# A decoder block's forward and backward pass: V of seven groups kept on chip, moments centred in PSUM, gradients staged over V and K

## The chip, the cores and the metric

The kernel runs on one core of a Trainium2 chip. The metric is the device time of one execution in microseconds (us). The kernel before takes 814.06 us, the median of three runs (812.51 to 818.42). Engines are named PE (TensorE's matmuls), PEld (its weight loads), DVE (VectorE), ACT (ScalarE), POOL (GpSimd) and SP (SyncE). POOL and SP compute little here; their queues issue the transfers.

## What is computed

One token of 448 features passes through attention over a key and value cache and a gated layer without a nonlinearity; the outputs are the result and the gradients of eight inputs. Cut to what matters:

```python
def f(x, k_cache, v_cache, wq, wo, w_gate, w_up, w_down):
    q = layernorm(x) @ wq                       # 16 heads of 256, 8 groups of 2 heads
    k = k_cache[:, :, Sk - 4096:, :]            # Sk = 32768: the last 4096 rows of each group
    v = v_cache[:, :, Sk - 4096:, :]
    p = softmax(q @ k.T / 16)                   # per head
    h = x + (p @ v).reshape(1, 4096) @ wo
    n = layernorm(h)
    return h + ((n @ w_gate) * (n @ w_up)) @ w_down
out, vjp = jax.vjp(f, ...)
return out, *vjp(grad_out)
```

All is bf16. The gradients of the two caches have the full shape (8, 32768, 256): outside the last 4096 rows they are zero, and these zeros must be written. That is 235 MB of the 281 MB that the kernel writes.

## The kernel before

**Two streams of transfers.** SP's queue (`FILL`) writes the zeros from a constant tile, 14,336 KB at a time, from the start on, without waiting for anything computed (lines 57 to 75). The last region is cut into pieces (`CUT`, line 72): most of it from all 128 partitions, 63 rows of 16 KB from 3 partitions (`LOW3`), and on POOL's queue, after the load of the up weights (`fill_rest`, line 77), 176 rows of 16 KB from 8 partitions (`HIGH8`) and a little from `LOW8`. POOL's queue (`IO`) carries all other transfers, in the order of its program: loads of K, V and weights, and stores of gradients. A transfer that waits for a buffer holds up those behind it. The order on each engine is laid out by a scheduler that may pull later work ahead of work that waits.

**Memory.** `S` has eight slots of 16 KB per partition, each for one group's window of K or V (4096 rows of 256, 32 rows `t` per partition). `K_SLOT` and `V_SLOT` (lines 31 and 32) say which. V of groups 5, 6 and 7 takes slots that K or other data need again, so `V_AGAIN` loads them a second time in the backward stage. `Mt` holds the moments in fp32; `Rt` is a ring of scratch buffers and later holds weights.

**Forward stage**, per group g of 8 (lines 365 to 383): `scores` transposes K in TensorE (line 283), evacuates by `evac`, which gives its copies to ACT and DVE by turns (lines 227 and 229), and multiplies by q. `softmax` follows. `moments` (line 325) forms for every t the product of K's rows with the two heads' probabilities (DVE, line 335) and accumulates in PSUM V^T (p K), a 256 x 512 matrix (line 339), which serves dq later: the gradient of q needs V^T diag(p) K without its mean part, o times kbar, where o = V^T p and kbar = K^T p. o and kbar are accumulated by four 128 x 2 matmuls per t (lines 342 and 345). `load_K(g + 2)` and `load_V(g + 1)` are issued ahead of the group's work.

**Middle**: attention's output `ao` by wo (line 401), loaded in two halves `woA` and `woB`; the gated layer (line 411); `spread` (line 419) brings a column vector to all partitions for the products that give gradients (lines 441 and 453); `dq_ps` (line 471) multiplies the moments with the gradient of o, and the mean part kbar times delta is subtracted.

**Backward stage**, per group: V is transposed again (line 586), evacuated and multiplied by the gradient of o (line 591); from it come 32 rows for outer products (line 604); 16 times two matmuls give dV and dK for two t each (line 620), evacuated into two of the four staging slots `STG`, and stored (line 625). Between the groups the `side` jobs make the weight gradients: `outer` (line 494) multiplies a row by scalars into one of two staging buffers in `Mt` and stores it. `dxn_load` and `dxn_part` (lines 526 and 530) load wq again and reduce it for dx; `ffn_out` (line 515) loads w_down again and gives the block's output.

Of the kernel before, what the change touches and what calls it, by code (L numbers as in the profile page):

```python
# [26 lines left out]
NS = 8  # L27
NV = 5
# [6 lines left out]
K_SLOT = [5, 6, 7, 5, 6, 7, 5, 7]  # L35
V_SLOT = [0, 1, 2, 3, 4, 6, 6, 5]
V_AGAIN = {5: 1, 6: 2, 7: 3}
# [3 lines left out]
def kernel(  # L41
# [8 lines left out]
    small = ctx.enter_context(tc.tile_pool(name="small", bufs=2))  # L50
    ps = ctx.enter_context(tc.tile_pool(name="ps", bufs=1, space=bass.MemoryType.PSUM))

    x_bf = const.tile([1, D], bf16, tag="rowa", name="x_bf")
    FILL.dma_start(out=x_bf[:], in_=A_x.rearrange("a b d -> (a b) d"))
    go_bf = const.tile([1, D], bf16, tag="rowb", name="go_bf")
    FILL.dma_start(out=go_bf[:], in_=grad_out.rearrange("a b d -> (a b) d"))
# [15 lines left out]
    CUT = [n * ZW for n in (0, 640, 656, 719, 720, 896)]  # L72
    fill(FILL, last[CUT[2]:CUT[3]], LOW3, 21, ZW)
    fill(FILL, last[CUT[0]:CUT[1]], ALL, 5, ZW)
    fill(FILL, last[CUT[1]:CUT[2]], ALL, 1, ZW // 8)

    def fill_rest():
        fill(IO, last[CUT[3]:CUT[4]], LOW8, 2, 512)
        fill(IO, last[CUT[4]:CUT[5]], HIGH8, 22, ZW)


    S = const.tile([128, NS, SLOT], bf16)
    Mt = const.tile([128, G, 2, 2 * Dh], f32)
    Rt = const.tile([128, SLOT], bf16)

    def slot(k):
        return S[:, k, :]

    def slot_kv(k):
        return S[:, k, :].rearrange("p (t d) -> p t d", d=Dh)  # L90
# [17 lines left out]
    wq_sb = S[:, 1:3, :].rearrange("p a b -> p (a b)")[:, 0:NI * HQ]  # L108
# [4 lines left out]
    wd0 = S[:, 3, 0:FC * D].rearrange("p (c n) -> p c n", n=D)  # L113
    IO.dma_start(out=wd0, in_=B_w_down.rearrange("(c p) n -> p c n", p=128))

# [5 lines left out]
    ones_bf = const.tile([128, 128], bf16)  # L121
    V_.memset(ones_bf[:], 1.0)
    ones_f = const.tile([128, 128], f32)
    V_.memset(ones_f[:], 1.0)
    eps_t = const.tile([128, 1], f32)
# [35 lines left out]
    def rows_to_half(row, xe):  # L161
        t = ps.tile([128, NI], f32, tag="tmp", bufs=1)
        for i in range(NI):
            c = xe[i // 4][:, (i % 4) * 128:(i % 4 + 1) * 128]
            V_.tensor_copy(out=c.rearrange("o (m r) -> o m r", r=2), in_=half_cols(row, i))
            P_.matmul(t[:, i:i + 1], lhsT=c, rhs=ones_f[0:1, 0:1], start=True, stop=True)
        return t
# [64 lines left out]
    xe0 = [Mt[0:1, G - 1, k, :] for k in range(2)]  # L232
    xX = const.tile([128, NI], f32)
    V_.tensor_copy(out=xX[:], in_=rows_to_half(x_bf[:], xe0)[:])
    gX = const.tile([128, NI], f32)
    V_.tensor_copy(out=gX[:], in_=rows_to_half(go_bf[:], xe0)[:])
# [24 lines left out]
    kbar = const.tile([128, 32], f32)  # L261
# [4 lines left out]

    def kt_buf():
        k = kt_ctr[0] % NB
        kt_ctr[0] += 1
        return Rt[:, k * 1024:(k + 1) * 1024].rearrange("p (i h c) -> p i h c", i=4, h=2)  # L270

    def pk_buf():
        k = NB + pk_ctr[0] % NB
        pk_ctr[0] += 1
        return Rt[:, k * 1024:(k + 1) * 1024].rearrange("p (i h d) -> p i h d", i=2, h=2)
# [24 lines left out]
    def softmax(g):  # L300
# [19 lines left out]
        pf = small.tile([128, T, 2], f32, tag="p_f")  # L320
# [4 lines left out]
    def moments(g):  # L325

        K, Vv, pf = Kw[g], Vw[g], p_f[g]
        MT = fps.tile([128, 2, 2 * Dh], f32, tag="MT", name="MT")
        acc = fps.tile([128, 8], f32, tag="acc", name="acc")
        for c in range(T // 2):  # L330
# [5 lines left out]
            for i in range(2):  # L336
                t = 2 * c + i
                for hf in range(2):
                    P_.matmul(MT[:, hf, :], lhsT=Vv[:, t, hf * 128:(hf + 1) * 128], rhs=pk[:, i, :, :].rearrange("p h d -> p (h d)"),  # L339
                              start=(t == 0), stop=(t == T - 1))  # L340
                for hf in range(2):
                    P_.matmul(acc[:, 2 * hf:2 * hf + 2], lhsT=Vv[:, t, hf * 128:(hf + 1) * 128], rhs=pT_all[:, g, t, :],  # L342
                              start=(t == 0 and hf == 0), stop=(t == T - 1), skip_group_check=True)
                for dk in range(2):
                    P_.matmul(acc[:, 4 + dk:7 + dk:2], lhsT=K[:, t, dk * 128:(dk + 1) * 128], rhs=pT_all[:, g, t, :],  # L345
                              start=False, stop=(t == T - 1), skip_group_check=True)
        S_.copy(out=Mt[:, g, 0, :], in_=MT[:, 0, :])  # L347
        V_.tensor_copy(out=Mt[:, g, 1, :], in_=MT[:, 1, :])
        V_.tensor_copy(out=oT_f[:, 4 * g:4 * g + 4].rearrange("p (h f) -> p f h", f=2), in_=acc[:, 0:4].rearrange("p (f h) -> p f h", h=2))
        V_.tensor_copy(out=kbar[:, 4 * g:4 * g + 4], in_=acc[:, 4:8])  # L350
        V_.tensor_copy(out=oT_bf[:, 4 * g:4 * g + 4], in_=oT_f[:, 4 * g:4 * g + 4])

    wo_v = A_wo.rearrange("(b p) n -> p b n", p=128)
    woA = S[:, 6, 0:16 * D].rearrange("p (b n) -> p b n", n=D)
    woB = S[:, 5, 0:16 * D].rearrange("p (b n) -> p b n", n=D)
    wg_sb = S[:, 7, 0:NI * HF]
    wu_sb = Rt[:, 0:NI * HF]
    bc2 = [S[:, 7, NI * HF:NI * HF + F].rearrange("p (i c) -> p i c", i=2), Rt[:, NI * HF:NI * HF + F].rearrange("p (i c) -> p i c", i=2)]

    def wo_b(b):  # L360
        return woA[:, b, :] if b < 16 else woB[:, b - 16, :]
# [3 lines left out]
    for g in range(G):  # L365
        if g + 1 < NV:
            load_V(g + 1)
        if g + 2 < 7:
            load_K(g + 2)
        if g == 5:  # L370
            load_V(5)
        if g == 6:
            load_V(6)
            load_K(7)
        if g == 7:
            load_V(7)
            IO.dma_start(out=woA, in_=wo_v[:, 0:16, :])
        softmax(g)
        if g + 1 < G and g != 6:
            scores(g + 1)  # L380
        moments(g)
        if g == 6:
            scores(7)
        if g == 0:

            t = ps.tile([128, D], f32, tag="tmp", bufs=1)
            P_.matmul(t[:], lhsT=ones_bf[0:1, :], rhs=go_bf[:], start=True, stop=True)
# [4 lines left out]
    IO.dma_start(out=woB, in_=wo_v[:, 16:32, :])  # L392
# [6 lines left out]
    ao = ps.tile([1, D], f32, tag="tmp", bufs=1)  # L399
# [3 lines left out]
    V_.tensor_tensor(out=hX[:], in0=rows_to_half(ao[:], [S[0:1, k, 16 * D:SLOT].bitcast(f32) for k in (5, 6)])[:], in1=xX[:], op=ALU.add)  # L403
    rstd2, xh2, xf2, xx2 = layernorm(hX[:], "ln2")

    gu_ps = fps.tile([128, 2, 2, NI], f32, tag="sT", bufs=2)
# [12 lines left out]
    def spread(dst, src, nb, rows2):  # L419

        for b0 in range(0, nb, 4):
            n = min(4, nb - b0)
            t = fps.tile([2, 4, 128], f32, tag="sT", bufs=2, name="t")
            for j in range(n):
                P_.matmul(t[:, j, :], lhsT=src[:, b0 + j:b0 + j + nb + 1:nb], rhs=ident_bf[:], start=True, stop=True)
            evac(rows2[:, b0 * 128:(b0 + n) * 128].rearrange("p (b c) -> p b c", b=n), t[:, 0:n, :])
        for i2 in range(2):
            for b0 in range(0, nb, 4):
                n = min(4, nb - b0) * 128
                t = fps.tile([128, 512], f32, tag="sT", bufs=2, name="t")  # L430
                P_.matmul(t[:, 0:n], lhsT=Par[:, i2, :], rhs=rows2[:, b0 * 128:b0 * 128 + n], start=True, stop=True)
                evac(dst[:, i2, b0 * 128:b0 * 128 + n], t[:, 0:n])

    rows2 = [S[0:2, k, 16 * D:16 * D + HF] for k in (5, 6)]
    for w in range(2):
        spread(bc2[w], dgu[:, w, :], NI, rows2[w])
    P2 = const.tile([128, 2, NI], f32)
    for w, w_sb in ((0, wg_sb), (1, wu_sb)):
        wv = w_sb.rearrange("p (i c) -> p i c", i=NI)
        for i in range(NI):  # L440
            V_.tensor_tensor_reduce(out=wv[:, i, :], in0=wv[:, i, :], in1=bc2[w][:, i % 2, :], scale=1.0, scalar=0.0,  # L441
                                    op0=ALU.mult, op1=ALU.add, accum_out=P2[:, w, i:i + 1])
    dhn = const.tile([128, NI], f32)
    V_.tensor_tensor(out=dhn[:], in0=P2[:, 0, :], in1=P2[:, 1, :], op=ALU.add)
    dhZ = layernorm_bwd(dhn[:], xh2[:], rstd2[:, 0:1], gX[:], 0.5, "dhZ")

    dh_ps = fps.tile([128, D], f32, tag="sT", bufs=2)
# [18 lines left out]
    dq_ps = fps.tile([128, 32], f32, tag="acc", name="dq_ps")  # L466
    for h in range(H):
        for dk in range(2):
            for hf in range(2):
                c0 = (h % 2) * Dh + dk * 128  # L470
                P_.matmul(dq_ps[:, 2 * h + dk:2 * h + dk + 1], lhsT=Mt[:, h // 2, hf, c0:c0 + 128], rhs=doT_f[:, 2 * h + hf:2 * h + hf + 1],  # L471
                          start=(hf == 0), stop=(hf == 1))
    kd = small.tile([128, H, 2], f32, tag="kd")
    V_.tensor_tensor(out=kd[:], in0=kbar[:].rearrange("p (h f) -> p h f", f=2), in1=delta[:].unsqueeze(2).to_broadcast([128, H, 2]), op=ALU.mult)
    dqd = small.tile([128, 32], f32, tag="dqd")
    V_.tensor_tensor(out=dqd[:], in0=dq_ps[:], in1=kd[:].rearrange("p h f -> p (h f)"), op=ALU.subtract)
    dq = const.tile([128, 32], bf16)
    V_.tensor_scalar(out=dq[:], in0=dqd[:], scalar1=SCALE, scalar2=None, op0=ALU.mult)
    late = Mt[:].rearrange("p g f c -> p (g f c)").bitcast(bf16)
    dq_bc = late[:, 0:2 * HQ].rearrange("p (i c) -> p i c", i=2)  # L480
    spread(dq_bc, dq[:], 16, late[0:2, 4096:6144])
    fps_cm.__exit__(None, None, None)
    st_ctr = [0]

    def stage_buf():
        k = 1 + st_ctr[0] % 2
        st_ctr[0] += 1
# [170 lines left out]
```

## Time and profile before

| | |
|---|---|
| median of the runs | 814.06 us |
| the profiled execution, its own time | 811.53 us |
| its span | 809.8 us |
| bytes moved | 338.58 MB (read 57.28, written 280.59) |
| mean granted clock of TensorE | 0.644 |
| PE busy | 493.9 us (61%) |
| DVE busy | 378.3 us (47%) |
| ACT busy | 166.4 us (21%) |
| last moment matmul ends | 322 us |
| stores of dV and dK of group 0, issued | 532 us |
| of group 7, issued | 797 us |

The page cuts the span into 40 slices of 20.2 us; each digit is a busy share in tenths, DMA the mean share of the 16 DMA engines, and GB/s what they moved. Lists of waits give the waiting instruction, what released it, the total in us, how often, and the longest. A line number is one of the kernel; `evac`'s lines are shared by all that call it, and there the tile's name tells who did.

### The profile page before, as it was taken

The numbers are of one execution on the slowest core, as the hardware profiler recorded it, in microseconds if no ns is written. First come the engines' busy times: TensorE is split into PE (matmuls) and PEld (weight loads), VectorE is DVE, ScalarE is ACT, GpSimd is POOL, SyncE is SP. The second block draws the span as 40 slices with busy tenths as digits, with TensorE's granted clock in tenths as the row PEclk, the third lists the DMA queues.
The fourth block names the chain that finished last, engine by engine and source line by source line (L and its number), as shares of the span: only waits on it lengthen the run. The fifth ranks groups of instructions, "written<-read, shape, count | busy, mean of one in ns | idle before, by whom it ended". The sixth has DMA issues, their size and how long they took to land.

```text
span 809.8 us, 11007 instructions
## 1 busy us (share of the span) xinstructions
PE 493.9 (61%) x4479; PEld 294.7 (36%) x4479; DVE 378.3 (47%) x1149; ACT 166.4 (21%) x261; POOL 41.6 (5%) x77
## 2 busy tenths in 40 slices
PE   3559959999647529034597888687043454437742
PEld 3555536666324405012595774325031111001110
DVE  4128738777446306006674325683151463425532
ACT  0230111222000200001003332343011232224421
POOL 3000000000000001000000001010010110000000
PEclk9959688999778758665555556555555555555555
DMA  8999999999999999999999999999999999999996
GB/s 343 431 427 424 430 429 429 428 426 426 431 426 427 419 428 426 411 429 429 428 428 430 414 424 420 430 417 431 423 425 420 409 416 417 428 424 427 423 397 274
DMA packets 24920, 338.58 MB, mean 418 GB/s; under 512 B 1485, under 2 KB 1551, under 8 KB 5047
## 3 DMA queue, kind: packets, MB, share of 16 engines
q1 hardware_dynamic: 14550, 231.98, 67.8%
q0 software_dynamic: 10320, 105.90, 31.3%
q8 instruction: 35, 0.57, 0.3%
q14 instruction: 15, 0.12, 0.0%
HBM read 57.28 MB, written 280.59 MB: 417 GB/s over the span
## 4 chain that ended last, share of the span: by engine, by line
issue 24%; DMA 15%; PE 13%; DVE 7%; another core or an unknown queue 3%; POOL 1%; ACT 1%; POOLq 0%; ACTq 0%; DVEq 0%
DMA S<-in_A_v_cache_dram 5%; DMA S<-in_A_wo_dram 4%; DMA out_dram<-Mt 4%; PE dq_ps L471 3%; PE d_ps L620 2%; DMA Rt<-in_A_wq_dram 2%; DVE Rt L530 2%; PE MT L339 2%; DVE S L229 2%; PE tr L586 1%; ACT S L227 1%; DVE Rt L441 1%; POOL out_dram L495 1%; PE dh_ps L176 1%
## 5 line engine op out<-in xcount | busy, mean ns | idle before, releaser
L620 PE MATMUL d_ps<-R,Mt 32*128 32x512 bf16 x256 | 120.1, 605 | 102.6 <-DVE S L229 101.6
L339 PE MATMUL MT<-Rt,S 128*128 128x512 bf16 x512 | 147.6, 401 | 29.0 <-DMA S<-in_A_v_cache_dram 29.0
L335 DVE TENSOR_SCALAR Rt<-S,pf 128x256 bf16<-128x256 bf16 x512 | 117.5, 282 | 57.0 <-PE MT L339 50.3
L229 DVE CAST S<-d_ps 128x512 bf16<-128x512 f32 x128 | 86.6, 689 | 62.8 <-ACT S L227 37.0
L227 ACT CAST S<-d_ps 128x512 bf16<-128x512 f32 x128 | 74.8, 586 | 155.2 <-PE d_ps L620 152.9
L620 PEld LDWEIGHTS <-Mt 32*128 32x128 bf16 x256 | 26.4, 115 | 175.8 <-issue 173.4
L342 PEld LDWEIGHTS <-S 128*128 128x128 bf16 x512 | 49.3, 100 | 60.7 <-issue 9.4
L283 PE MATMUL tr<-ident_bf,S 128*128 128x128 bf16 x512 | 49.7, 256 | 34.0 <-DMA S<-in_A_k_cache_dram 29.6
L586 PE MATMUL tr<-ident_bf,S 128*128 128x128 bf16 x512 | 66.3, 307 | 1.9 <-ACT Mt L227 1.2
L586 PEld LDWEIGHTS <-S 128*128 128x128 bf16 x512 | 49.8, 139 | 9.6 <-issue 9.5
L283 PEld LDWEIGHTS <-S 128*128 128x128 bf16 x512 | 39.0, 116 | 32.5 <-DMA S<-in_A_k_cache_dram 30.0
L342 PE MATMUL acc<-pT_all,S 128*128 128x2 bf16 x512 | 48.2, 166 | 0.0
L345 PE MATMUL acc<-pT_all,S 128*128 128x2 bf16 x512 | 47.5, 164 | 0.0
L339 PEld LDWEIGHTS <-S 128*128 128x128 bf16 x512 | 33.8, 98 | 35.7 <-DMA S<-in_A_v_cache_dram 29.8
L227 ACT COPY Rt<-tr 128x1024 bf16<-128x1024 bf16 x32 | 32.4, 1012 | 65.3 <-PE tr L283 65.0
L227 ACT COPY Mt<-tr 128x1024 bf16<-128x1024 bf16 x32 | 32.4, 1013 | 62.0 <-PE tr L586 35.9
L347 ACT COPY Mt<-MT 128x512 f32<-128x512 f32 x8 | 4.7, 585 | 192.5 <-PE MT L339 165.2
L229 DVE COPY Mt<-tr 128x1024 bf16<-128x1024 bf16 x32 | 22.1, 690 | 41.6 <-PE tr L586 41.5
L401 PE MATMUL ao<-S,oT_bf 128*1 128x448 bf16 x32 | 9.4, 461 | 46.3 <-DMA S<-in_A_wo_dram 46.3
L229 DVE COPY Rt<-tr 128x1024 bf16<-128x1024 bf16 x32 | 22.1, 689 | 31.6 <-PE tr L283 30.4
L345 PEld LDWEIGHTS <-S 128*128 128x128 bf16 x512 | 31.0, 97 | 0.3 <-issue 0.3
L591 PEld LDWEIGHTS <-Mt 128*128 128x128 bf16 x512 | 20.2, 108 | 24.4 <-ACT Mt L227 12.5
(183 smaller groups left out, 451.5 us busy)
## 6 DMA issues: line engine op xcount, KB each, us to landing
out_dram<-zeros SPq DMA_DIRECT2D x15, 14336.0 KB, 148.9
out_dram<-S POOLq DMA_DIRECT2D x16, 2048.0 KB, 29.7
S<-in_A_v_cache_dram POOLq DMA_DIRECT2D x11, 2048.0 KB, 42.7
S<-in_A_k_cache_dram POOLq DMA_DIRECT2D x8, 2048.0 KB, 27.9
out_dram<-zeros SPq DMA_DIRECT2D x1, 10240.0 KB, 138.4
out_dram<-Mt POOLq DMA_DIRECT2D x6, 896.0 KB, 26.0
S<-in_A_wq_dram POOLq DMA_DIRECT2D x1, 3584.0 KB, 14.6
S<-in_A_wo_dram POOLq DMA_DIRECT2D x2, 1792.0 KB, 31.9
```

The lines of the kernel that those rows point to most:

```text
L227: S_.copy(out=out, in_=in_)
L229: V_.tensor_copy(out=out, in_=in_)
L283: P_.transpose(tr[:, i, dh, :], Xw[:, 4 * q + i, dh * 128:(dh + 1) * 128], ident_bf[:])
L335: V_.tensor_scalar(out=pk[:, i, h, :], in0=K[:, t, :], scalar1=pf[:, t, h:h + 1], scalar2=None, op0=ALU.mult)
L339: P_.matmul(MT[:, hf, :], lhsT=Vv[:, t, hf * 128:(hf + 1) * 128], rhs=pk[:, i, :, :].rearrange("p h d -> p (h d)"), start=(t == 0), stop=( ...
L342: P_.matmul(acc[:, 2 * hf:2 * hf + 2], lhsT=Vv[:, t, hf * 128:(hf + 1) * 128], rhs=pT_all[:, g, t, :], start=(t == 0 and hf == 0), stop=(t ...
L345: P_.matmul(acc[:, 4 + dk:7 + dk:2], lhsT=K[:, t, dk * 128:(dk + 1) * 128], rhs=pT_all[:, g, t, :], start=False, stop=(t == T - 1), skip_g ...
L471: P_.matmul(dq_ps[:, 2 * h + dk:2 * h + dk + 1], lhsT=Mt[:, h // 2, hf, c0:c0 + 128], rhs=doT_f[:, 2 * h + hf:2 * h + hf + 1], start=(hf = ...
L530: V_.tensor_tensor_reduce(out=wq2[:, i - i0, :], in0=wq2[:, i - i0, :], in1=dq_bc[:, i % 2, :], scale=1.0, scalar=0.0, op0=ALU.mult, op1=A ...
L586: P_.transpose(tr[:, i, dh, :], Vw[g][:, 4 * q + i, dh * 128:(dh + 1) * 128], ident_bf[:])
L591: P_.matmul(dp[:, 4 * q + i, :], lhsT=xt[:, i, dh, :], rhs=doT[:, 4 * g + dh:4 * g + dh + 3:2], start=(dh == 0), stop=(dh == 1))
L620: P_.matmul(d_ps[:, i, :, :].rearrange("p w d -> p (w d)"), lhsT=rows[32 * k:32 * k + 32, a, :], rhs=R[32 * k:32 * k + 32, :], start=True, ...
```

## The change

- V of groups 0 to 6 has a slot each, and is loaded once; V of group 7 takes a slot of K after `moments(6)` and is loaded again in the backward stage, after group 1's stores, into the slot of V of group 0. K has two slots by turns; `load_K(g + 2)` is issued after `moments(g)`. V of groups 1 and 2 is loaded with the first transfers, the next ones three groups ahead.
- One allocation `BIG` holds the slots and the scratch rings, with offsets by hand (`BASE`). `Mt` is bf16. `small` tiles have one buffer but for a few.
- In `moments` o and kbar come from one matmul per t, with the two probabilities as weights and V's and K's row of t side by side (two matmuls for groups 5 and 6, where the two slots are too far apart). Their product is subtracted in PSUM by two matmuls per group with a negated kbar, before `Mt` is evacuated, so that the subtraction after `dq_ps` goes.
- wo is loaded whole after the last moments, with w_gate and w_up behind it. `spread` leaves its result in PSUM, which the reductions read; ScalarE copies it to `bc2` afterwards.
- dV is staged over V of its group, dK over K's slot `g % 2`. The 12 pieces of the weight gradients have buffers of their own: `spare` in `Mt`, and halves of slots that are dead by then, and are dealt to other groups. `ffn_out` moves to group 3, the reduction of wq to groups 4 and 5.
- The fill pieces of the last region are cut anew.

The core of the diff:

```diff
-K_SLOT = [5, 6, 7, 5, 6, 7, 5, 7]
-V_SLOT = [0, 1, 2, 3, 4, 6, 6, 5]
-V_AGAIN = {5: 1, 6: 2, 7: 3}
+KS = 7
+TAIL = 6 * SLOT
+TEND = TAIL + 10496
+SIZE = TEND + 3 * SLOT
+BASE = [3 * SLOT, TEND, 2 * SLOT, TEND + SLOT, SLOT, TEND + 2 * SLOT, 0, 4 * SLOT, 5 * SLOT]
+K_SLOT = [KS + g % 2 for g in range(G)]
+V_SLOT = [0, 1, 2, 3, 4, 5, 6, KS]
...
-    CUT = [n * ZW for n in (0, 640, 656, 719, 720, 896)]
-    fill(FILL, last[CUT[2]:CUT[3]], LOW3, 21, ZW)
+    CUT = [n * ZW // 16 for n in (0, 10240, 11264, 11376, 12144, 12160, 14336)]
+    fill(FILL, last[CUT[3]:CUT[4]], LOW3, 16, ZW)
     fill(FILL, last[CUT[0]:CUT[1]], ALL, 5, ZW)
-    fill(FILL, last[CUT[1]:CUT[2]], ALL, 1, ZW // 8)
+    fill(FILL, last[CUT[1]:CUT[2]], ALL, 1, ZW // 2)
+    fill(FILL, last[CUT[2]:CUT[3]], ALL, 1, 448)
...
-        fill(IO, last[CUT[4]:CUT[5]], HIGH8, 22, ZW)
+        fill(IO, last[CUT[5]:CUT[6]], HIGH8, 17, ZW)
...
     load_K(1)
+    load_V(1)
-    wd0 = S[:, 3, 0:FC * D].rearrange("p (c n) -> p c n", n=D)
+    wd0 = slot(5)[:, 0:FC * D].rearrange("p (c n) -> p c n", n=D)
     IO.dma_start(out=wd0, in_=B_w_down.rearrange("(c p) n -> p c n", p=128))
+    load_V(2)
...
-                for hf in range(2):
-                    P_.matmul(acc[:, 2 * hf:2 * hf + 2], lhsT=Vv[:, t, hf * 128:(hf + 1) * 128], rhs=pT_all[:, g, t, :],
...
-                for dk in range(2):
-                    P_.matmul(acc[:, 4 + dk:7 + dk:2], lhsT=K[:, t, dk * 128:(dk + 1) * 128], rhs=pT_all[:, g, t, :],
...
+                if hi - lo < 4 * SLOT:
+                    x = BIG[:, lo + t * Dh:lo + (t + 1) * Dh]
+                    both = bass.AP(x.tensor, x.offset, [x.ap[0], [hi - lo, 2], x.ap[1]])
+                    P_.matmul(acc[:], lhsT=pT_all[:, g, t, :], rhs=both, start=(t == 0), stop=(t == T - 1))
+                else:
+                    for k, x in enumerate((Vv, K) if at[0] == lo else (K, Vv)):
+                        P_.matmul(acc[:, k, :], lhsT=pT_all[:, g, t, :], rhs=x[:, t, :], start=(t == 0 and k == 0), stop=(t == T - 1), skip_group_check=True)
+        iv = at.index(lo)
+        S_.copy(out=orow, in_=acc[:, iv, :])
+        V_.tensor_tensor(out=kneg.rearrange("p (h d) -> p h d", h=2), in0=acc[:, 1 - iv, :].unsqueeze(1).to_broadcast([2, 2, Dh]),
+                         in1=neg2[:].unsqueeze(2).to_broadcast([2, 2, Dh]), op=ALU.mult)
+        for hf in range(2):
+            P_.matmul(MT[:, hf, :], lhsT=orow[:, hf * 128:(hf + 1) * 128], rhs=kneg, start=False, stop=True, skip_group_check=True)
...
     for g in range(G):
-        if g + 1 < NV:
-            load_V(g + 1)
-        if g + 2 < 7:
-            load_K(g + 2)
...
+        if g + 3 < G - 1:
+            load_V(g + 3)
         softmax(g)
-        if g + 1 < G and g != 6:
+        if g + 1 < G:
             scores(g + 1)
         moments(g)
-        if g == 6:
-            scores(7)
+        if g + 2 < G:
+            load_K(g + 2)
+        if g + 2 == G:
+            load_V(G - 1)
...
-    IO.dma_start(out=woB, in_=wo_v[:, 16:32, :])
+    IO.dma_start(out=wo_sb, in_=A_wo.rearrange("(b p) n -> p b n", p=128))
...
     side = {
-        0: [o67_job(0, 0, 4), o67_job(0, 4, 7), lambda: dxn_part(0, 4), lambda: dxn_load(4, 7)],
-        1: [lambda: dxn_part(4, 7), dx_out],
-        2: [o5_job(0), o5_job(8)],
-        3: [o5_job(16), o5_job(24)],
-        4: [lambda b=b: outer(o8, b, b + 7, lambda n: dh2_bc[:], hh, D) for b in (0, 7)],
-        5: [o4_job(0), o4_job(2)],
-        6: [o4_job(4), o4_job(6)],
+        0: [o67_job(spare, 0, 4, 7)],
+        1: [o5_job(spare, 0), lambda: load_window(slot_kv(0), A_v_cache, G - 1)],
+        2: [o5_job(spare, 8), wd_load],
+        3: [ffn_out, o5_job(spare, 16), lambda: dxn_load(0, 4)],
+        4: [lambda: dxn_part(0, 4), o5_job(half(1, 0), 24), lambda: dxn_load(4, 7)],
+        5: [lambda: dxn_part(4, 7), dx_out, o8_job(half(1, 1), 0), o8_job(spare, 7)],
+        6: [o4_job(half(2, 0), 0), o4_job(half(2, 1), 2), o4_job(half(3, 0), 4), o4_job(half(3, 1), 6)],
         7: [],
     }
-    ffn_out()
-    o67_job(1, 0, 4)()
-    o67_job(1, 4, 7)()
-    dxn_load(0, 4)
+    o67_job(spare, 1, 0, 4)()
+    o67_job(half(8, 0), 1, 4, 7)()
+    o67_job(half(8, 1), 0, 0, 4)()
...
-        sv = slot_kv(STG[(2 * g) % 4])
-        sk = slot_kv(STG[(2 * g + 1) % 4])
-        stg = [sv, sk]
+        stg = [Vw[g], Kw[g]]
```

## The prediction

> **What bounds the kernel now.** I read the slices of the span first, since they say whether anything but the transfers can matter:
>
> ```profile
> PEclk9959688999778758665555556555555555555555
> DMA  8999999999999999999999999999999999999996
> GB/s 343 431 427 424 430 429 429 428 426 426 431 426 427 419 428 426 411 429 429 428 428 430 414 424 420 430 417 431 423 425 420 409 416 417 428 424 427 423 397 274
> DMA packets 24920, 338.58 MB, mean 418 GB/s; under 512 B 1485, under 2 KB 1551, under 8 KB 5047
> ...
> q1 hardware_dynamic: 14550, 231.98, 67.8%
> q0 software_dynamic: 10320, 105.90, 31.3%
> ```
>
> The 16 DMA engines are full from the second slice to the 38th, at 411 to 431 GB/s, whatever the compute engines do. Two queues feed them: SP's (q1, the zero fills, 232 MB, no dependence on anything computed) and POOL's (q0, all else). When POOL's is empty the fills take the whole rate; so a stall in the computation costs no time of its own as long as fills are left. Only the first slice and the last two are short of bytes. The busy time by stretch shows by how much:
>
> ```profile
> 20.00:784.00 764.00, 477.46 (x4428) 285.66 (x4429) 361.49 (x1092) 159.02 (x249) 33.34 (x54) 0.64 1.01 425
> 784.00:797.00 13.00, 8.94 (x20) 1.90 (x18) 7.35 (x11) 5.85 (x10) 0.53 (x1) 0.50 0.58 248
> 797.00:808.00 11.00, 0.00 (x0) 0.00 (x0) 0.00 (x0) 0.00 (x0) 0.53 (x1) 0.50 0.90 381
> ```
>
> The last three columns are clock, DMA share and GB/s. Until 784 us all is full. From 784 to 797 the fills run out while the last group is still being computed, and 42% of the DMA time is unused (13 x 0.42 = 5.5 us). From 797 the last two stores go out alone. The chain of waits (start, length, what) says the same from the other side: it ends with the issue of the last group's stores, and its long pieces are loads and stores, but for dq's matmuls.
>
> ```profile
> 320.44 35.91 DMA S<-in_A_wo_dram
> ...
> 401.24 25.88 PE dq_ps L471 x120
> ...
> 496.95 19.04 DMA Rt<-in_A_wq_dram
> ...
> 696.00 32.81 DMA out_dram<-Mt
> ...
> 796.31 0.53 POOL out_dram L625
> ```
>
> So there are two ends: that of the bytes and that of the chain of computation (797 us plus the landing). Now the chain is last by a little. The sum needs both. For the chain I read the waits of VectorE from 439 us on, the waits of TensorE, and the DMA issues (KB each, us to landing):
>
> ```profile
> DVE Mt L494 <- DMA out_dram<-Mt: 51.8, 8, 14.8
> DVE Rt L530 <- DMA Rt<-in_A_wq_dram: 27.3, 2, 22.1
> DVE S L229 <- DMA out_dram<-S: 25.1, 4, 9.7
> ...
> PE MT L339 <- DMA S<-in_A_v_cache_dram: 29.0, 3, 14.9
> ...
> PE tr L283 <- DMA S<-in_A_k_cache_dram: 29.6, 3, 11.7
> ...
> S<-in_A_v_cache_dram POOLq DMA_DIRECT2D x11, 2048.0 KB, 42.7
> S<-in_A_k_cache_dram POOLq DMA_DIRECT2D x8, 2048.0 KB, 27.9
> ...
> Rt<-in_B_w_down_dram POOLq DMA_DIRECT2D x1, 1568.0 KB, 25.4
> ```
>
> **The bytes.** V is loaded 11 times (8, and groups 5, 6, 7 again); afterwards 9 times (8, and group 7 again). K, wq, wo, wd and all stores keep their bytes; the fill pieces are cut anew but add up to the same 14,336 KB for the last region (10,240 + 1,024 + 112 + 768 + 16 + 2,176). So 2 x 2,048 KB = 4.19 MB go. At the 425 GB/s of 20 to 784 us: -9.9 us (between 4.19/431 = 9.7 and 4.19/409 = 10.3).
>
> The Trainium skill (DMA: Bandwidth & Descriptors, Specifications) gives about 358 GB/s as the HBM limit of one core, which would make this 11.7 us and the result 1.8 us lower; the 425 GB/s here are above it, so the trace disagrees and its rate is used.
>
> **The tail.** If the chain ends before the fills do, the 5.5 us of 784 to 797 are filled: -5.5. In their place comes what the fills leave uneven. Besides the even pieces, 3 partitions get 16 rows of 16 KB (were 21) and 8 others 17 (were 22). One row takes an engine 16,384 B / (425/16 GB/s) = 0.62 us, so 17 are 10.5. If these 11 partitions are on 11 engines, the other 5 end 10.5 us early, 5/16 x 10.5 = 3.3 us in the mean; if the 5 have other work instead, nothing is lost. The page shows such work, the instruction queue (q8, 0.3% of 16 engines' span, 39 us of one engine), but not where it lies. I take the middle, +1.5, and keep 0 and 3.3.
>
> [...]
>
> **The chain in the forward stage**, to be held against 797 us:
> - Loads. V1 to V3 are issued at the start, past the wd load and the K loads on POOL's queue. K has two slots instead of three: the load of K(g+2) is issued after moments(g), where it was a group earlier. What is queued behind its wait on POOL is the next V load, and late becomes scores(g+2), then softmax. Each of the six loads costs TensorE between 0 (moments(g+1), about 18 us of matmuls, is ready and fills the time) and 27.9 us (median landing, if scores stand first in TensorE's order). Shortest landing of a window is 15.9; the trace shows both orders (transposes of later groups run ahead of waiting ones at 447 to 488 us), so I take half of that, 8 each, 48; V7 behind moments(6) 16. They replace 29.0 + 29.6 of waits: +5 (bounds -43 and +125).
> - wo becomes one load after moments(7). In pieces of 896 B, as wo is, the wd load brought 1.61 MB in 25.4 us, 63 GB/s: 3.67 MB take 58 us, not 35.9: +22; gate and up weights (3.2 MB) queue behind it, +3 (bounds for both 0 and +37). The last fill pieces stay behind them on POOL's queue, 5 rows shorter.
> - o and kbar: 1,024 matmuls of 2 columns (48.2 + 47.5 us busy) become 192 of 512 and 128 of 256 columns; at 377 ns (median of the MT matmuls) 72 + 24 = 96. Nothing.
> - Centring: per group a copy (0.6), a product (0.7) and two fp32 matmuls of 512 columns (0.4 as in bf16, 1.5 at four times that) stand between the last moment matmul and the evacuation: 2.1 to 4.3 each. Scores of the next group can cover it. Half of 8 x 3.2: +13 (0 and +34).
> - spread reads PSUM, which spares eight evacuations (0.55 to 0.7 each): -4. dq in bf16 must wait for all of doT (32 x 0.71 = 22.6 us of VectorE), then 64 short matmuls, some 3 us, against 25.9: nothing.
>
> Together +39.
>
> **The chain in the backward stage** takes 439 to 797 us now, 45 per group. dV goes over V[g] itself and waits for no store; dK still has two slots; the 12 outer-product pieces have more buffers; wd and wq are loaded a group before they are used, where the 38 and 19 us before 516 us wait for them. The 51.8, 25.1 and 27.3 us of VectorE's waits are what can go, 104 in all, and the 57 before group 0. Floor: POOL still moves 53 MB (stores 33.6, the outer products 12.1, loads 7.4). The shortest interval between two groups' stores (747.0 to 767.9) moved 4.19 MB beside fills, 200 GB/s; 53 MB at that is 265 us, 33 per group. I take this, -93 (bounds -93 and 0). The last stores are then issued at 797 + 39 - 93 = 743 us, and fills last to about 793. The stores need 11 us, so they must be out by 782: 39 us to spare. Every chain cost above is therefore hidden behind fills.
>
> **The sum.** Profiled execution 811.53 (span 809.8, 1.7 around it): 811.5 - 9.9 - 5.5 + 1.5 = 797.6. The runs shown stand above it: the lowest 1.0, the median (814.06) 2.5. I add 1.4, about the middle less a little for a chain that no longer ends the kernel: 799.0. Of the forecast alone the range is 791 to 806: low with no unevenness and the fills at 431 GB/s instead of 425 where POOL is silent, high with half the tail kept and 2.5 for the median.
>
> **Rivals.**
> - The chain stays last, a little shorter. dK's two slots and one spare buffer used by five pieces make VectorE wait as now, and the backward stage saves half, 47. Last stores at 797 + 39 - 47 = 789; 811.5 - 8 = 803.5 plus the median's 2.5, 806; with a third saved 822. For it: the stores' landing of 29.7 us median is as long as a group. Against it: V reloads, which shared that queue, are mostly gone. 807 to 822: chance 0.13.
> - The other side: K's second slot. If TensorE has scores(g+2) ahead of moments(g+1), each of six loads is paid at 22 us (between 15.9 and 27.9) instead of 8: +84. Last stores at 743 + 84 = 827, the time 842. It decides from 39 us over my sum on (14.5 per load), and is slower than now by over 1% from about 63 (18.4 per load). For it: a K load is wanted right after it is issued. Against: 18 us of ready moments. Chance 0.10.
> - The rate itself moves. Slices in which POOL is silent run at 427 to 431 GB/s, those with small pieces at 409 to 420; if the new order mixes them otherwise, 1% of 790 us, 8 us, goes either way: 791 or 807. Against it: the same pieces are moved. Chance 0.05, half of it each way.
>
> That leaves 0.72 for the forecast. A measurement of this kernel tells about 1% from no change, 8 us: faster is below 806. Faster is the forecast and the better half of the last rival, 0.74; within 1% most of the first rival and the other half of the last, 0.14; slower the second rival and the rest of the first, 0.12. The range goes down to 790 and up to 818, over most of the first rival, which leaves some 0.17 outside.
>
> **What would show it.** Total bytes 334.4 MB and nine V loads; the DMA row full to the last slice but one; the fills, not the stores of the last group, ending last; the last stores issued well before 782 us; VectorE's waits on staging buffers at less than half of 104 us; the wait for wo longer than 36 us. I am wrong if the last slices show a low DMA share with TensorE still busy: then the chain is last, and the start of the first transposes after each K load tells whether K's slots did it.

## The result, and the profile after

The kernel after takes 860.68 us (median, 859.4 to 866.83) against 814.37 before (812.51 to 818.42, one more run than shown above): 1.0577 of it, interval 1.0512 to 1.0641. It is 46 us slower, where 15 us faster was forecast. The spans of the profiled executions are 857.6 and 809.8 us.

The page of the kernel after, its rows of the 40 slices (21.4 us each now):

```profile
PE   3569209869595977879391025416998978765672
...
DMA  8999999999999999999999999999999678567844
GB/s 345 431 424 430 430 432 429 429 429 432 427 429 429 427 424 431 421 429 431 425 430 414 426 430 427 431 431 427 425 426 424 282 275 344 244 253 277 349 196 196
DMA packets 24659, 334.28 MB, mean 390 GB/s; under 512 B 1413, under 2 KB 1623, under 8 KB 4975
```

The bytes are what was forecast (334.28 MB, V loaded nine times), and up to the 31st slice the transfers run as fast as before. Then the fills are used up, at 686 us, with a fifth of the span still to come, and the DMA engines wait for the computation, with TensorE busy for 5 to 9 tenths until the last slice. The chain is last by far. The two kernels by stretch, cut at the end of the moments, at the first store of dV and dK and at the last (and, after, at the end of the fills); columns: stretch, length, busy us of PE, PEld, DVE, ACT and POOL, TensorE's clock, DMA share, GB/s. Before:

```profile
0.00:322.00 322.00, 228.58 (x2768) 149.78 (x2769) 171.16 (x708) 45.09 (x76) 16.47 (x36) 0.83 1.00 422
322.00:532.00 210.00, 133.15 (x1162) 99.67 (x1160) 91.54 (x230) 44.74 (x59) 7.74 (x13) 0.56 1.01 424
532.00:797.00 265.00, 132.14 (x552) 45.23 (x550) 115.60 (x212) 76.58 (x126) 16.88 (x27) 0.50 0.99 413
```

After:

```profile
0.00:450.00 450.00, 318.35 (x2072) 132.78 (x2100) 180.84 (x709) 47.73 (x83) 13.57 (x33) 0.83 1.00 424
450.00:633.00 183.00, 80.06 (x691) 46.73 (x690) 70.60 (x186) 32.90 (x44) 5.71 (x8) 0.54 1.01 426
633.00:686.00 53.00, 50.19 (x560) 34.39 (x558) 24.53 (x49) 23.44 (x30) 1.61 (x3) 0.50 0.88 368
686.00:845.00 159.00, 114.97 (x422) 37.07 (x419) 110.85 (x199) 65.57 (x110) 18.60 (x29) 0.53 0.66 261
```

The forward stage takes 450 us instead of 322, +128. The middle takes 183 instead of 210, and first to last store 212 instead of 265: -80 together. 128 - 80 = 48, the difference of the spans. The clock, 0.83 in both forward stages, did not do it. In the last two stretches the transfers leave 53 x 0.12 + 159 x 0.34 = 60 us of DMA time unused; 857.6 - 60 is 798, close to the forecast of the bytes.

Two things grew in the forward stage. The groups of the kernel after (busy us, mean ns | idle before them, what ended most of it), and its waits and issues:

```profile
L360 PE MATMUL acc<-BIG,pT_all 128*2 128x512 bf16 x192 | 74.6, 392 | 4.8 <-DVE pT_all L336 3.3
...
L297 PE MATMUL tr<-ident_bf,BIG 128*128 128x128 bf16 x512 | 50.2, 260 | 86.1 <-DMA BIG<-in_A_k_cache_dram 84.2
```

```profile
PE tr L297 <- DMA BIG<-in_A_k_cache_dram: 84.2, 8, 36.4
...
PE ao L420 <- DMA BIG<-in_A_wo_dram: 53.8, 1, 53.8
...
PE MT L355 <- DMA BIG<-in_A_v_cache_dram: 11.0, 1, 11.0
```

```profile
out_dram<-BIG POOLq DMA_DIRECT2D x16, 2048.0 KB, 10.6
BIG<-in_A_v_cache_dram POOLq DMA_DIRECT2D x9, 2048.0 KB, 55.4
BIG<-in_A_k_cache_dram POOLq DMA_DIRECT2D x8, 2048.0 KB, 16.7
```

TensorE waits 84.2 us for K (29.6 before), eight times. Its timeline has each wait in the bracket at the end of the line (idle time before the instruction, and what ended it). The first four are:

```profile
26.84 1.67 PE L297 MATMUL tr<-ident_bf,BIG 128*128 128x128 bf16 x14 [11.32 <-DMA BIG<-in_A_k_cache_dram]
48.72 0.50 PE L297 MATMUL tr<-ident_bf,BIG 128*128 128x128 bf16 x3 [9.46 <-DMA BIG<-in_A_k_cache_dram]
128.66 1.89 PE L297 MATMUL tr<-ident_bf,BIG 128*128 128x128 bf16 x16 [36.36 <-DMA BIG<-in_A_k_cache_dram]
183.21 1.89 PE L297 MATMUL tr<-ident_bf,BIG 128*128 128x128 bf16 x16 [5.74 <-DMA BIG<-in_A_k_cache_dram]
```

The first two, for K of groups 0 and 1, were there before the change too (11.65 and 9.24 us). New is the third, 36.4 us for K of group 2: its load was issued at 88 us, behind loads of V that were issued at 32 us and took some 81 us to land. The five after it are of 5.1 to 5.8 us. The chain of waits from one load of K to the next shows one group (start, length, what):

```profile
262.09 16.28 DMA BIG<-in_A_k_cache_dram
278.42 1.89 PE tr L297 x16
...
304.47 5.09 issue
309.57 16.20 DMA BIG<-in_A_k_cache_dram
```

and TensorE's timeline what it does meanwhile:

```profile
263.01 1.98 PE L369 MATMUL MT<-BIG 2*128 2x512 f32 x4 [0.43 <-DVE BIG L366]
...
267.40 0.59 PE L192 MATMUL t<-sums,ones_f 128*128 128x2 f32 x2 [0.99 <-ACT e L331]
268.81 1.01 PE L360 MATMUL acc<-BIG,pT_all 128*2 128x512 bf16 x2 [0.82 <-DVE pT_all L336]
...
272.49 0.61 PE L355 MATMUL MT<-BIG 128*128 128x512 bf16 x2
278.42 1.46 PE L297 MATMUL tr<-ident_bf,BIG 128*128 128x128 bf16 x12 [5.32 <-DMA BIG<-in_A_k_cache_dram]
```

A group takes 47.5 us, from the issue of one load of K to the next. The load can start only when the moments of the group before have ended. In its 16.3 us TensorE does the centring and the small matmuls of a softmax, each of which waits for VectorE or ScalarE, and three of 32 `t` of the next moments; then the transposes stand first in its order and it waits. The second growth is inside the moments. Two stretches of TensorE's timeline, before and after:

```profile
315.26 0.59 PE L339 MATMUL MT<-Rt,S 128*128 128x512 bf16 x2
315.69 0.19 PE L342 MATMUL acc<-pT_all,S 128*128 128x2 bf16 x2
315.74 0.19 PE L345 MATMUL acc<-pT_all,S 128*128 128x2 bf16 x2
315.79 0.59 PE L339 MATMUL MT<-Rt,S 128*128 128x512 bf16 x2
```

```profile
295.69 0.60 PE L355 MATMUL MT<-BIG 128*128 128x512 bf16 x2
296.23 0.38 PE L360 MATMUL acc<-BIG,pT_all 128*2 128x512 bf16 x1
296.54 0.60 PE L355 MATMUL MT<-BIG 128*128 128x512 bf16 x2
```

Read the starts, not the lengths: one `t` takes 0.53 us before and 0.85 after. The lengths overlap, the distance of the starts is what a matmul costs. Two matmuls of 512 columns take 2 x 0.216 us in both. The four small matmuls start 25 ns apart and cost 0.10 us together; the row matmul costs 0.41. Over 256 `t`, 0.31 each is 80 us. In groups 5 and 6, where it is two matmuls of 256 columns, a `t` takes the same 0.85.

### The profile page after: what moved, and what is told of

Read it like the earlier page. It is cut to its first block, busy times and chain, and to the rows that moved or that the text cites. A ratio compares the mean times of both kernels' runs of the same rounds, so it can differ in the third digit from the quotient of the medians.

```text
span 857.6 us, 9464 instructions
## 1 busy us (share of the span) xinstructions
PE 563.6 (66%) x3731; PEld 251.0 (29%) x3759; DVE 386.8 (45%) x1142; ACT 169.6 (20%) x265; POOL 40.0 (5%) x74
## 2 busy tenths in 40 slices
DMA packets 24659, 334.28 MB, mean 390 GB/s; under 512 B 1413, under 2 KB 1623, under 8 KB 4975
## 4 chain that ended last, share of the span: by engine, by line
PE 35%; issue 13%; DVE 10%; DMA 10%; another core or an unknown queue 6%; ACT 4%; POOL 0%; POOLq 0%; ACTq 0%; DVEq 0%
PE MT L355 8%; DMA BIG<-in_A_k_cache_dram 8%; PE d_ps L631 7%; PE tr L602 5%; ACT BIG L237 3%; PE acc L360 3%; DVE BIG L239 3%; PE tr L297 2%; DVE BIG L471 2%; DMA BIG<-in_A_v_cache_dram 2%; PE acc L363 2%; PE dp L607 2%; DVE BIG L545 2%; DVE BIG L458 2%
## 5 line engine op out<-in xcount | busy, mean ns | idle before, releaser
L355 PE MATMUL MT<-BIG 128*128 128x512 bf16 x484 | 156.6, 403 | 13.2 <-DMA BIG<-in_A_v_cache_dram 11.0
L351 DVE TENSOR_SCALAR BIG<-BIG,pf 128x256 bf16<-128x256 bf16 x512 | 119.1, 283 | 75.2 <-PE MT L355 64.8
L631 PE MATMUL d_ps<-BIG 32*128 32x512 bf16 x256 | 120.3, 601 | 32.7 <-DVE BIG L239 31.3
L239 DVE CAST BIG<-d_ps 128x512 bf16<-128x512 f32 x128 | 87.2, 690 | 55.7 <-ACT BIG L237 55.5
L297 PE MATMUL tr<-ident_bf,BIG 128*128 128x128 bf16 x512 | 50.2, 260 | 86.1 <-DMA BIG<-in_A_k_cache_dram 84.2
L237 ACT COPY BIG<-tr 128x1024 bf16<-128x1024 bf16 x64 | 64.8, 1012 | 202.5 <-PE tr L297 158.7
L239 DVE COPY BIG<-tr 128x1024 bf16<-128x1024 bf16 x64 | 44.2, 690 | 118.2 <-PE tr L297 90.4
L237 ACT CAST BIG<-d_ps 128x512 bf16<-128x512 f32 x128 | 74.9, 587 | 88.5 <-PE d_ps L631 88.5
L360 PE MATMUL acc<-BIG,pT_all 128*2 128x512 bf16 x192 | 74.6, 392 | 4.8 <-DVE pT_all L336 3.3
L602 PE MATMUL tr<-ident_bf,BIG 128*128 128x128 bf16 x512 | 66.6, 302 | 8.2 <-ACT BIG L237 7.5
L297 PEld LDWEIGHTS <-BIG 128*128 128x128 bf16 x512 | 39.0, 118 | 89.2 <-DMA BIG<-in_A_k_cache_dram 86.9
L602 PEld LDWEIGHTS <-BIG 128*128 128x128 bf16 x512 | 47.6, 135 | 25.4 <-issue 25.4
L355 PEld LDWEIGHTS <-BIG 128*128 128x128 bf16 x512 | 32.1, 100 | 74.0 <-issue 62.8
L607 PEld LDWEIGHTS <-BIG 128*128 128x128 bf16 x512 | 20.8, 108 | 25.1 <-ACT BIG L237 16.7
## 6 DMA issues: line engine op xcount, KB each, us to landing
out_dram<-BIG POOLq DMA_DIRECT2D x16, 2048.0 KB, 10.6
```

The costliest lines, as they stand in the source:

```text
L237: S_.copy(out=out, in_=in_)
L239: V_.tensor_copy(out=out, in_=in_)
L297: P_.transpose(tr[:, i, dh, :], Xw[:, 4 * q + i, dh * 128:(dh + 1) * 128], ident_bf[:])
L351: V_.tensor_scalar(out=pk[:, i, h, :], in0=K[:, t, :], scalar1=pf[:, t, h:h + 1], scalar2=None, op0=ALU.mult)
L360: P_.matmul(acc[:], lhsT=pT_all[:, g, t, :], rhs=both, start=(t == 0), stop=(t == T - 1))
L602: P_.transpose(tr[:, i, dh, :], Vw[g][:, 4 * q + i, dh * 128:(dh + 1) * 128], ident_bf[:])
```

## Experiments

Four theories. 1: the row matmul. 2: K's second slot. 3: the forward stage's length decides the end, one for one. 4: it does not, because the backward stage's waits for transfers come back once fills run beside it. Each ratio is to the kernel before, run on the same chip.

**Four small matmuls again (small_acc)**, the rest as after; the mean part is subtracted after dq, as before:

```diff
-P_.matmul(acc[:], lhsT=pT_all[:, g, t, :], rhs=both, ...)   # 128x512, or two of 128x256
+for hf in range(2): P_.matmul(acc[:, 2*hf:2*hf+2], lhsT=Vv[:, t, hf*128:(hf+1)*128], rhs=pT_all[:, g, t, :], ...)
+for dk in range(2): P_.matmul(acc[:, 4+dk:7+dk:2], lhsT=K[:, t, dk*128:(dk+1)*128], rhs=pT_all[:, g, t, :], ...)
```

> The changed kernel with o and kbar again from four 128 x 2 matmuls per t, and without the centring in PSUM: kbar times delta is subtracted after dq as before. The rest stays, two K slots among it. Theory 1 (the row matmul is the cause: a row t of the moments takes 0.88 us of TensorE instead of 0.53, 8 x 32 x 0.35 = 90 us): the forward stage ends 90 to 110 us earlier than the 449 us of the changed kernel, the last stores are out before 782 us, the fills end last, 797 to 804 us. Theory 2 (K's second slot is the cause: a group lasts as long as the K load, scores and moments in a row): the freed time is spent waiting for K; the forward stage ends at 400 us or later and the time is 825 to 850.

Measured 835.18 us, 1.0231 (1.0198 to 1.0264). A `t` takes 0.533 us again, and the moments end at 366 instead of 450: -84. The end gains 23 of it (last store 821 instead of 844). By stretch, cut at the moments, the first store, the end of the fills and the last store:

```profile
366.00:550.00 184.00, 78.50 (x692) 46.79 (x693) 69.20 (x187) 32.44 (x43) 5.63 (x8) 0.53 1.01 427
550.00:739.00 189.00, 111.66 (x821) 54.92 (x820) 75.97 (x160) 56.34 (x83) 11.76 (x18) 0.53 1.00 414
739.00:821.00 82.00, 54.48 (x142) 15.56 (x141) 59.79 (x87) 32.64 (x56) 7.96 (x14) 0.52 0.55 224
```

First to last store now takes 271 us, 59 more than after, of which 189 beside fills (53 after). Its waits show what came back; neither stands in the list of after:

```profile
DVE Mt L500 <- DMA out_dram<-Mt: 31.2, 3, 12.3
PE t L524 <- DMA BIG<-in_B_w_down_dram: 29.3, 1, 29.3
```

Theory 1 holds for the forward stage, though -84 is just short of the 90 expected, and the time lies in the range that was named for theory 2. Theory 3 falls, theory 4 stands.

**No centring (no_centre)**, the two fp32 matmuls and their product left out, and with them the mean part of dq:

```diff
-V_.tensor_tensor(out=kneg..., in0=acc[:, 1 - iv, :]..., in1=neg2[:]..., op=ALU.mult)
-for hf in range(2): P_.matmul(MT[:, hf, :], lhsT=orow[:, hf*128:(hf+1)*128], rhs=kneg, start=False, ...)
```

> The changed kernel without the two fp32 matmuls per group that centre the moments and the product before them; the mean part of dq is left out. Theory 1: TensorE's time per group sets the forward stage, 2 to 3 us less in each of 8 groups, 16 to 24 us in all: 837 to 846 us. Theory 2: the K load is issued before the centring and lands after it, so nothing is won: 855 to 862.

Measured 848.22 us, 1.039 (1.034 to 1.0439); the moments end at 438, -12 us, and the last store at 832, -12. The time lies between the two ranges expected. A `t` still takes 0.845 us: the row matmul, not the centring, is the larger part of theory 1.

**Three slots for K (three_k, small_acc_three_k)**, as before the change, so that a load starts a group earlier; V of group 6 is loaded in group 5's turn.

> The changed kernel with three K slots by turns: K takes slot 6 for groups 2 and 5, and V of group 6 is loaded into it after moments(5); dK is staged as in the changed kernel. The row matmul and the centring stay. Theory 1: a group of the forward stage still needs 28 us for moments, 8 for scores and 3 for the centring, 39 to 41 instead of 47.7; 800 to 835 us, the chain last, a row t still 0.85 to 0.88 us. Theory 2: the forward stage is back to 35 us per group and the fills end last: 797 to 804.

> Both of the former: four 128 x 2 matmuls per t, no centring in PSUM, and three K slots. Both theories: the forward stage ends at 300 to 340 us, the fills end last, and the time is what the bytes give, 795 to 803 us, faster than the kernel before. If it is above 810, a third cause is at work, the late load of wo or the waits of the backward stage.

Measured 850.24 us, 1.0403 (1.0361 to 1.0446), and 825.6 us, 1.0105 (1.0068 to 1.0142). In both, the load of K of group 2 stands ahead of q's matmuls, whose wq lies in the same slot, so that q is formed from K's data and its matmuls start at 96 us instead of 28. Both times lie outside the ranges expected, and they say nothing of the price of the second slot; two more runs have that load behind q:

```diff
-K_SLOT = [KS + g % 2 for g in range(G)]
+K_SLOT = [7, 8, 6, 7, 8, 6, 7, 8]
...
+        if g == 0:
+            load_K(2)
...
-        if g + 2 < G:
-            load_K(g + 2)
+        if g + 3 < G:
+            load_K(g + 3)
...
-        stg = [Vw[g], Kw[g]]
+        stg = [Vw[g], slot_kv(KS + g % 2)]
```

> The changed kernel with three K slots, K of group 2 loaded after q has been formed (in the run before, it was ahead of q's matmuls, which made the first group some 60 us late). Row matmul and centring stay. Theory 1 (the row matmul holds the forward stage): 38 to 40 us per group, moments end at 385 to 405 us instead of 450, and of these 50 us some 30% arrive at the end, as the 85 us of small_acc brought 25: 840 to 848. Theory 2 (K's slots hold it): moments end at 330 to 350 us, 805 to 830.

> Four 128 x 2 matmuls per t, no centring in PSUM, three K slots, K of group 2 loaded after q. Moments should end at 285 to 300 us, 35 us before the kernel before. Theory 3 (the forward stage decides, and what it gains arrives at the end until the fills are last): 797 to 805 us. Theory 4 (beside the fills the backward stage's own waits, for w_down in ffn_out and for the spare buffer, grow by what the forward stage gains): last stores still at 795 to 805, 808 to 820 us.

Three slots alone: 839.79 us, 1.0334 (1.0311 to 1.0357); the moments end at 403, -47, the last store at 824, -20. Both parts: 806.93 us, 0.9925 (0.9899 to 0.9951); the moments end at 311.5, -138.5, a little more than 84 + 47 (285 to 300 was expected), and the last store at 792, -52. Theories 1 and 2 together explain the forward stage, and again less than half of what it gains arrives. The time lies between what theories 3 and 4 expected. From the end of the moments to the last store this kernel takes 480 us, after takes 394, before 475. Its waits for transfers in the backward stage (from 480 us on):

```profile
DVE Mt L504 <- DMA out_dram<-Mt: 38.1, 3, 16.3
...
PE t L528 <- DMA BIG<-in_B_w_down_dram: 30.5, 1, 30.5
...
DVE BIG L543 <- DMA BIG<-in_A_wq_dram: 12.0, 2, 9.2
```

These and four smaller ones on transfers come to 103 us, much like the 104 before the change; the kernel after has none behind its wait for wo.

**The side jobs dealt later (redealt)**, on top of both parts: `ffn_out` in group 4 instead of 3, the two reductions of wq one group later each.

```diff
-3: [ffn_out, o5_job(spare, 16), lambda: dxn_load(0, 4)],
-4: [lambda: dxn_part(0, 4), o5_job(half(1, 0), 24), ...],
-5: [lambda: dxn_part(4, 7), dx_out, o8_job(half(1, 1), 0), ...],
+3: [o5_job(spare, 16), lambda: dxn_load(0, 4)],
+4: [ffn_out, o5_job(half(1, 0), 24), ...],
+5: [lambda: dxn_part(0, 4), o8_job(half(1, 1), 0), ...],
+6: [lambda: dxn_part(4, 7), dx_out, ...
```

> small_acc_three_k_v2 with the side jobs dealt later: ffn_out one group after its load of w_down is issued (after group 4, not 3), the two reductions of wq after groups 5 and 6. Theory 4: TensorE's wait of some 30 us for w_down goes, and the last stores are 25 to 35 us earlier than in small_acc_three_k_v2, until the fills are last: 797 to 803 us. Theory 3: within 4 us of small_acc_three_k_v2.

Measured 800.56 us (800.11 to 800.63), 0.9848 (0.9827 to 0.9869): faster than both kernels, by 1.5% against before, and than the one without the new dealing. The wait for w_down falls from 30.5 to 12.3 us, and the last store comes 12 us earlier, where 25 to 35 were expected. Its bytes and its last stretches, cut at the first store, the end of the fills, the last store and the end:

```profile
DMA packets 24664, 334.37 MB, mean 419 GB/s; under 512 B 1413, under 2 KB 1623, under 8 KB 4975
```

```profile
494.00:770.00 276.00, 162.72 (x947) 69.84 (x945) 129.02 (x239) 84.01 (x130) 19.35 (x31) 0.50 1.01 420
770.00:781.00 11.00, 6.98 (x16) 1.48 (x14) 5.88 (x9) 4.69 (x8) 1.06 (x2) 0.50 0.90 379
781.00:797.00 16.00, 0.00 (x0) 0.00 (x0) 0.00 (x0) 0.00 (x0) 0.00 (x0) 0.50 0.68 288
```

Fills and chain end within 11 us of each other, and 1 us of DMA time is unused between them; behind the last store 16 x 0.32 = 5 us more are.

**Wide weights for the row matmul (wide_weights)**: the kernel after, with 128 columns of V as weights in place of the two probabilities; o, kbar and what follows from them have other values.

```diff
-P_.matmul(acc[:], lhsT=pT_all[:, g, t, :], rhs=both, ...)
+P_.matmul(acc[:], lhsT=Vv[:, t, 0:128], rhs=both, ...)
```

> The changed kernel, but the row matmul has 128 columns of V as weights instead of the two probabilities; o and kbar become sums of V's products, so the values differ, the number and length of matmuls does not. If a matmul of two weight columns makes TensorE's pipeline wait at the change to 128 columns and back, a row t of the moments falls from 0.85 to 0.65 us (three matmuls at 0.215): moments end 45 to 55 us earlier. If three matmuls of 512 columns just take 0.85 us there, it stays at 0.85.

One run, 841.48 us, where before took 812.87; the moments end at 398, -52. The timeline of TensorE, with its weight loads (PEld):

```profile
390.23 0.59 PE L355 MATMUL MT<-BIG 128*128 128x512 bf16 x2
390.45 0.10 PEld L360 LDWEIGHTS <-BIG 128*128 128x128 bf16 x1
390.66 0.38 PE L360 MATMUL acc<-BIG 128*128 128x512 bf16 x1
390.88 0.59 PE L355 MATMUL MT<-BIG 128*128 128x512 bf16 x2
```

A `t` takes 0.65 us, three times 0.216: 512 columns each, with no gap. So of the row matmul's 0.41 us, 0.216 are its columns, and 0.197 come with weights of two columns among weights of 128. The weight loads show where. Here the load for the row matmul starts at 390.45, 0.21 us ahead of its matmul and beside the one before. In the kernel after, the two loads next to the row matmul shown above are

```profile
296.23 0.08 PEld L360 LDWEIGHTS <-pT_all 128*2 128x2 bf16 x1 [0.42 <-issue]
296.54 0.11 PEld L355 LDWEIGHTS <-BIG 128*128 128x128 bf16 x2 [0.23 <-issue]
```

Both start together with their matmul (296.23 and 296.54), not ahead of it: about 0.1 us is lost on either side.

**Each part alone, put into the kernel before (rows_in_before, two_k_in_before)**:

```diff
+P_.matmul(acc[:], lhsT=pT_all[:, g, t, :], rhs=both, ...)    # rows_in_before, in place of the four
...
-K_SLOT = [5, 6, 7, 5, 6, 7, 5, 7]
+K_SLOT = [5, 6, 5, 6, 5, 6, 5, 7]                            # two_k_in_before, load_K(g + 2) behind moments(g)
```

> The kernel before with the row matmul alone: o and kbar from one matmul of two weight columns per t (two matmuls of 256 for groups 0 to 2, where the slots are far apart), turned into columns by four small transposes per group; moments in fp32, not centred, three K slots, V loaded 11 times. Theory 1: a row t takes 0.85 us instead of 0.53, 10 us per group; moments end 30 to 85 us later than 322 (the 59 us of waits for loads can take up the rest), and since the chain is last already, 825 to 850 us. If the row matmul is harmless by itself: 810 to 818.

> The kernel before with two K slots alone: K of group g + 2 is loaded after moments(g) into the slot of K of group g, V of group 5 has the slot that comes free; the rest stays. Theory 2: scores of the next group wait for the load in each of five groups, 7 to 12 us more per group, moments end 35 to 60 us later, 820 to 840 us. If K's slots are harmless by themselves: 810 to 818.

Measured 842.69 us, 1.0341 (1.0303 to 1.0379), and 840.7 us, 1.0314 (1.0273 to 1.0355). The moments end at 395 and 387 instead of 322. Rows: the wait for K falls, that for V grows. Slots: the wait for K is nearly that of the kernel after.

```profile
PE MT L339 <- DMA S<-in_A_v_cache_dram: 43.6, 3, 22.9
...
PE tr L283 <- DMA S<-in_A_k_cache_dram: 20.8, 2, 11.9
```

```profile
PE tr L283 <- DMA S<-in_A_k_cache_dram: 80.5, 8, 26.4
```

Either part makes the kernel before slower by 25 to 27 us at the end, for 65 to 73 in the forward stage.

**Where the gain goes.** Six of these kernels are variants of the kernel after whose moments end earlier. Set against it, in us, the last column being all waits of TensorE, VectorE and ScalarE for transfers from 440 us on, without that for wo (the kernel after has none):

| kernel | moments earlier | last store earlier | lost between | waits come back |
|---|---|---|---|---|
| no_centre | 12 | 12 | 0 | 1 |
| three_k_v2 | 47 | 20 | 27 | 30 |
| wide_weights | 52 | 18 | 34 | 41 |
| small_acc | 84 | 23 | 61 | 71 |
| small_acc_three_k_v2 | 138.5 | 52 | 86 | 98 |
| redealt | 140 | 65 | 75 | 75 |

What is lost is close to the waits that come back, and the first 12 us arrive in full.

## Why the prediction was wrong

**Right: the bytes.** 334.28 MB were moved, and where the chain ends only 11 us after the fills (redealt) the kernel takes 800.56 us. Against before on its chip that is -12.3 us; the sum of the bytes and the tail gave -13.9. That it comes so near is in part luck: the tail's -4 isn't shown by any run. redealt leaves 11 x 0.10 + 16 x 0.32 = 6 us of DMA time unused at its end, as much as before (13 x 0.42 + 11 x 0.10 = 6.6). wo waited as the row of w_down said: 57.0 us to landing, 58 forecast. Centring cost 12 us in the forward stage, forecast 13.

**Wrong, the first step: "o and kbar ... 96. Nothing."** It measured +72 in the forward stage (the 84 of small_acc less the 12 of no_centre), and 80 by the starts. The error is that I priced both sides by busy time, though the lengths overlap. The small matmuls, 48.2 + 47.5 us busy, cost 0.10 x 256 = 26 by their starts. The row matmul, at the 377 ns that its neighbours are busy, came to 96 and costs 0.41 x 256 = 105: near by luck, since by its starts such a neighbour costs 0.216, and the rest is the gap around two-column weights, of which I knew nothing. The Trainium skill (TensorE: Matmul & The Clock Gate, Back-to-back issue gap) states a floor of about 25 ns from start to start for up to 64 columns, and about 216 ns for an isolated matmul of 512. For a stream of weight loads and matmuls of 512 columns the same section gives about 131 ns. This trace agrees with the first two, at 25 and 216 ns, and not with the third: its stream runs at 216 too. By the first two figures the step would have been 256 x (0.216 - 0.10) = +30 us, as an estimate; the other 50 are the gap, which only the runs show.

**Wrong, the second step: the loads, at "8 each", that "replace 29.0 + 29.6 of waits".** They were forecast at +5 against before. K and V were waited for 84.2 + 11.0 us, 36.6 more than the 29.6 + 29.0 before, and giving K its third slot back took 47 us off the forward stage. Most of the error is in what was to be replaced: 20.9 of the 29.6 us are the waits for K of groups 0 and 1, which the change doesn't touch. Without them the same sum gives 64 - 37.7 = +26. The 18 us of ready moments that were to fill the time did not: the softmax stands ahead of them and was itself uncovered, three `t` ran, and then the transposes came first, as the rival on K's slot had it. The six loads cost 63.4 us instead of 48: five of them 5.1 to 5.8, less than the 8 that I took, and the first alone 36.4, K of group 2 queued behind the early loads of V. That rival named the place, though at the end K's slot alone was worth 21 to 25 us, not 43.

Together: 18 us were forecast up to the end of the moments (loads and centring), 128 measured; 80 for the row matmul, 12 for the centring and 36.6 of waits add up to it.

**Wrong, and hidden by the other two: the backward stage, "33 per group. I take this, -93", and "39 us to spare".** From the end of the moments to the last store the sum implies 475 + 25 - 4 - 93 = 403 us, and the kernel after took 394. That looks right by luck: my rate was one beside fills, and here there were none for the last 159 us: dV and dK landed in 10.6 us (median), not 29.7. Where fills run on, the stretch takes 480 (both parts undone) and 470 (redealt), against 475 before, and the waits on transfers are back at 103 and 78 us. Beside fills the change shortens the backward stage by next to nothing: staging over V and K frees slots, but loads and stores that share the engines with fills are still late. So even with the forward steps right the 39 us to spare were not there: where the moments end at 311.5 and 310, earlier than forecast, the last stores are issued 27 us (both parts undone) and 11 us (redealt) after the end of the fills.

This coupling is also why +128 became +46. The total of bytes is fixed: what the forward stage loses, fills use, and the backward stage then runs without them and faster. It is why 138 us won back in the forward stage give 52 at the end. That the returning waits take the rest is borne out by the six kernels of the table. That it is the fills that bring the waits back fits the landing of the stores (28.6 us in redealt, 10.6 in the kernel after), but is argued: no run took the fills away by themselves.

**What stays open**: why two-column weights cost 0.197 us among wide ones. The timelines show that neither weight load at the switch runs ahead of its matmul; what holds it back, no run here tells.

## What to carry to other kernels

Price matmuls by the distance of their starts in the timeline, never by busy time: short ones overlap, and a change of weight shape can cost nearly as much as 512 columns do (0.197 against 0.216 us here). Before a wait is counted as replaced, look at when it falls. When a buffer is taken away, look at what stands ahead of the work that is meant to cover the later load, and whether that work is itself ready. Beside a background stream a stage's speed depends on when the stream ends, so a gain for one stage can't be added to a loss in another: compare both at the same state of the stream.

## What the runs showed of the hardware

A matmul with weights of two columns and 512 columns of data takes 0.41 us between matmuls with weights of 128 columns, and 0.216 us with weights of 128 columns itself. With two columns the weight load starts with its matmul, with 128 columns 0.21 us ahead of it. Four matmuls of two columns of data between those of 512 add 0.10 us. The same 2 MB store lands in 10.6 us (median) where the fills have mostly ended, and in 28.6 beside them.
